# Dense 128-wide query and key products in a fused two-block attention kernel, with half of the x tiles transposed by DMA

## The chip, the cores and the metric

The kernel runs on one core of one Trainium2 chip. The metric is device time in microseconds (us) for one launch; a run's time is that of its slowest core, and here there is one. Engines are named as in the profile: PE (TensorE, matmuls; PEld its weight loads), ACT (ScalarE), DVE (VectorE), POOL (GpSimd) and SP (SyncE, which here only issues DMAs).

## The reference

Two independent blocks over 2048 tokens of width 640 with 32 heads of 20 dimensions; the outputs stand side by side.

```python
def _A_ref(x, wqkv, wo):                     # softmax attention
    qkv = (x @ wqkv).reshape(B, S, 3, H, Dh) # B=1, S=2048, H=32, Dh=20
    scores = einsum("bhqd,bhkd->bhqk", q, k) * Dh ** -0.5
    p = softmax(scores, axis=-1)
    o = einsum("bhqk,bhkd->bhqd", p, v)
    return o.reshape(B, S, D) @ wo           # D=640
def _B_ref(x, wqkv, wo):                     # linear attention
    phi = lambda t: where(t > 0, t + 1, exp(t)) + 1e-6
    kv = einsum("bhsd,bhse->bhde", phi(k), v); z = phi(k).sum(s)
    o = (phi(q) @ kv) / (phi(q) @ z + 1e-6)
    return o.reshape(B, S, D) @ wo
return concatenate([A, B], axis=-1)          # (1, 2048, 1280), bfloat16
```

## The kernel before

**Block A, the bulk.** The heads are taken in 8 groups of four, the queries in 4 chunks of 512 (qc), the keys in 16 tiles of 128 (kt). A block n is one query chunk and one group; there are 32, and n = 8 qc + g. The score of one head, 128 keys and 512 queries is a matmul of 32 rows (20 dimensions and padding) that fills one PSUM bank; four heads lie on the four row groups of PE and run side by side. There are 2048 such units. Most go to ACT, which takes the exponential of two banks at a time (`exp_op`, L1797, 128x1024, 746 instructions over PSUM banks 0 to 3); 556 of them go through DVE (L1695) and POOL (L1871), which form the exponential from three shifted integer copies. Then PE multiplies by V (`pv_emit`), DVE and POOL normalize (`norm`), small DMAs collect the heads (`f_OTd<-f_OTn`, L1919), and an output product follows.

**Projections.** Group 0 and group 1 (`_NP = 2`) have weights padded to 32 columns a head (`wqp`, `wkp`), so that their products (`step_qk0`) land in the layout that the scores want. The other 24 heads are computed 6 at a time, 120 columns wide (`_CH`, `step_qk`), evicted by DVE to a buffer `f_sq`, and each head is sent to its place by a DMA of 20 rows x 512 (L1175). So each 512 tokens take 2 + 4 products for queries and as many for keys: 48 in all, each of 5 quads (a quad is four matmuls of 32 columns side by side). x is needed transposed (`f_xT`): the 16 tiles of 128 tokens are loaded by four large DMAs and turned on PE (5 transposes a tile, L1031 and L949) with a copy by DVE or ACT behind (L1038, L1041, L1094).

**Block B** runs in PE's free time: its steps (`b_steps`) are held back by a pace, so that step k starts when a share between `B0` = 0.26 and `B1` = 0.92 of A's exponentials is scored. On ACT it has 52 exponentials (L1316). Its loads start in `begin`, once all K and V are there; `begin` makes DVE, ACT, POOL and SP wait (`barrier`) for the last users of the memory that it takes over.

**The order** is made when the program is built. `run` walks the engines along estimated times and emits what is ready; each engine then runs its list strictly in order, with semaphores between engines. On PE, `try_pe` tries a score burst first, then the step in hand, PV, more steps, and fillers that read zeros (`f_zt`). Score bursts may run at most two ahead of the exponentials. Projection steps wait in the list `qa` with a due block; those due within two blocks of the current one are urgent.

## Time and profile before

| quantity | value |
|---|---|
| median of 3 runs (lowest, highest) | 756.52 us (756.34, 756.85) |
| the profiled execution: time, span | 757.82 us, 755.7 us |
| busy: PE, ACT, DVE, POOL | 738.3, 712.1, 606.4, 584.2 us |
| mean granted clock of PE | 0.996 |

The span runs from the first to the last instruction; 2.1 us of the profiled execution lie around it. A busy share is a mean over stages, so the views of the rows below go by time: which engine idles when, and what it waits for.

### The profile page before, as it was taken

To read this page: it belongs to the slowest core of one execution; us is meant where nothing else is said; L and a number is where in the kernel's file an instruction comes from. 1 tells how busy PE (TensorE), PEld (TensorE's weight loads), DVE (VectorE), ACT (ScalarE), POOL (GpSimd) and SP (SyncE) were. 2 spreads that over 40 slices of the span, in tenths; PEclk is the share of its full clock that TensorE was granted. 3 is DMA by queue.
4 is the path that set the end of the run, shared out by engine and by line. 5 is a ranking of instruction groups with operands and counts; after the bars stand their busy time and mean duration, and the time that the engine had idled before them with its cause. 6 is when DMAs were issued, how large, how long until landed. Compare 5 with 4: busy or idle time off the path is not lost.

```text
span 755.7 us, 25131 instructions
## 1 busy us (share of the span) xinstructions
PE 738.3 (98%) x10955; PEld 263.4 (35%) x10955; DVE 606.4 (80%) x1158; ACT 712.1 (94%) x806; POOL 584.2 (77%) x344
## 2 busy tenths in 40 slices
PE   7999999999899999999999999999999999999996
PEld 4533442333223333333333333233233332333334
DVE  5788778877687788888888788798888787998982
ACT  4579889999999999999999999999999999999994
POOL 6468755779878788887879888877988878798781
PEclk9999999999999999999999999999999999999999
DMA  9101111105201002001000003020010100010001
GB/s 310 28 3 26 26 29 29 29 22 132 42 15 35 5 9 50 7 23 24 3 7 21 30 7 101 10 46 15 23 41 15 37 32 18 10 35 15 15 19 48
DMA packets 38494, 26.32 MB, mean 35 GB/s; under 512 B 21356, under 2 KB 38380, under 8 KB 38380
## 3 DMA queue, kind: packets, MB, share of 16 engines
q1 hardware_dynamic: 37068, 24.27, 11.6%
q8 instruction: 87, 1.43, 0.8%
q10 hardware_dynamic: 1312, 0.41, 0.2%
q14 instruction: 27, 0.22, 0.1%
HBM read 9.58 MB, written 5.24 MB: 20 GB/s over the span
## 4 chain that ended last, share of the span: by engine, by line
ACT 61%; PE 35%; DVE 2%; DMA 1%; POOL 0%; issue 0%; ACTq 0%; SPq 0%; DVEq 0%; POOLq 0%
ACT f_PT L1797 58%; PE ps L155 34%; ACT ps L1316 2%; DMA f_ar<-in_A_wqkv_dram 1%; DVE f_Sr L1695 1%; DVE f_KT L1118 0%; DVE f_xT L1094 0%; PE ps L949 0%; POOL f_Sr L1871 0%; DMA f_KT<-f_sq 0%; DVE f_ar L1350 0%; DVE f_V L1210 0%; DVE f_xT L1038 0%; DVE f_ar L1318 0%; DVE f_sq L1178 0%
## 5 line engine op out<-in xcount | busy, mean ns | idle before, releaser
L1797 ACT ACTIVATE f_PT<-ps 128x1024 bf16<-128x1024 f32 x746 | 698.3, 1128 | 29.6 <-PE ps L155 29.3
L1871 POOL TENSOR_SCALAR f_Sr<-f_Sr 128x2048 int16<-128x2048 int16 x278 | 527.5, 1898 | 108.4 <-PE ps L155 82.3
L1695 DVE TENSOR_SCALAR f_Sr<-ps 128x512 int16<-128x512 f32 x556 | 377.5, 684 | 77.0 <-PE ps L155 69.5
L155 PE MATMUL ps<-f_Qr,f_KT 32*128 32x512 bf16 x2048 | 293.4, 384 | 7.0 <-ACT f_PT L1797 3.6
L155 PEld LDWEIGHTS ps<-f_Qr,f_KT 32*128 32x128 bf16 x2048 | 74.1, 91 | 251.2 <-ACT f_PT L1797 227.6
L155 PE MATMUL ps<-f_ar 128*32 128x320 bf16 (+3 forms) x2496 | 156.1, 310 | 0.2
L155 PE MATMUL ps<-f_PT,f_V 128*21 128x512 bf16 x1492 | 142.8, 383 | 0.0
L155 PE MATMUL ps<-f_Sr,f_V 128*21 128x512 bf16 x1112 | 102.6, 382 | 0.0
L155 PEld LDWEIGHTS ps<-f_ar 128*32 128x32 bf16 (+1 forms) x2496 | 59.2, 95 | 69.1 <-issue 43.6
L1894 POOL TENSOR_TENSOR f_T<-f_T,f_Rt 128x512 bf16<-128x512 f32 x31 | 32.5, 1048 | 35.5 <-DVE f_Rt L1892 33.6
L155 PE MATMUL ps<-f_Sr,f_Vp 128*21 128x512 bf16 x556 | 54.5, 382 | 0.0
L155 PEld LDWEIGHTS ps<-f_PT,f_V 128*21 128x21 bf16 x1492 | 36.7, 90 | 46.2 <-issue 37.4
L1318 DVE SCALAR_TENSOR_TENSOR f_ar<-ps,f_ar 128x320 bf16<-128x320 f32 (+1 forms) x52 | 29.3, 563 | 12.5 <-ACT ps L1316 11.0
L155 PE MATMUL ps<-f_xT,f_ar 128*32 128x512 bf16 x480 | 37.4, 390 | 0.2
L155 PEld LDWEIGHTS ps<-f_Sr,f_V 128*21 128x21 bf16 x1112 | 25.6, 90 | 30.3 <-issue 20.3
L155 PE MATMUL ps<-f_ar,f_xT 128*32 128x160 bf16 x1280 | 34.8, 234 | 0.4 <-DVE f_Sr L1695 0.3
L1316 ACT ACTIVATE ps<-ps 128x320 f32<-128x320 f32 (+1 forms) x52 | 32.7, 629 | 0.0
L1314 DVE TENSOR_SCALAR f_ar<-ps 128x320 f32<-128x320 f32 (+1 forms) x52 | 28.8, 554 | 2.1 <-PE ps L155 2.1
L1901 DVE STREAM_TRANSPOSE f_T<-ps 128x512 f32<-128x512 f32 x32 | 22.7, 708 | 8.9 <-PE ps L155 8.7
L155 PEld LDWEIGHTS ps<-f_ar,f_xT 128*32 128x32 bf16 x1280 | 23.4, 96 | 14.4 <-issue 7.1
L155 PE MATMUL ps<-f_wo,f_OTd 120*32 120x320 bf16 x512 | 27.4, 302 | 0.0
L155 PE MATMUL ps<-f_xT,f_wq 128*32 128x512 bf16 (+1 forms) x320 | 24.6, 383 | 0.0
(78 smaller groups left out, 361.9 us busy)
## 6 DMA issues: line engine op xcount, KB each, us to landing
out_dram<-f_st SPq DMA_DIRECT2D x32, 160.0 KB
f_ar<-in_B_wqkv_dram SPq DMA_DIRECT2D x3, 800.0 KB
f_ar<-in_A_x_dram SPq DMA_DIRECT2D x3, 640.0 KB
f_Qr<-f_sq SPq DMA_DIRECT2D x96, 20.0 KB
f_KT<-f_sq SPq DMA_DIRECT2D x96, 20.0 KB
f_OTd<-f_OTn SPq DMA_DIRECT2D x96, 20.0 KB
f_ar<-in_A_wqkv_dram SPq DMA_DIRECT2D x2, 800.0 KB
f_wq<-in_A_wqkv_dram SPq DMA_DIRECT2D x1, 800.0 KB
```

The lines of the kernel that those rows point to most:

```text
L155: lambda e: e.matmul(out, lhsT, rhs, start=start, stop=stop, tile_position=tp, skip_group_check=sgc),
L1314: self.push("dve", lambda e: e.tensor_scalar(r1, src, 0.0, 1e-6, op0=ALU.max, op1=ALU.add), (("ps", b),), (rk,), _c_dve(n), prio=1, ok=ok, ...
L1316: "act", lambda e: e.activation(src, src, AF.Exp), (), (("ps", b),), _c_act(n), prio=0,
L1318: "dve", lambda e: e.scalar_tensor_tensor(dst, src, 1.0, r1, op0=ALU.min, op1=ALU.add),
L1695: post = lambda: self.push("dve", lambda e: e.tensor_scalar(self.Sr[:, s, i, :], self.ps[:, b, :], 0.0, 32639.0 - self.PH[-1], op0=ALU.max ...
L1797: return _Op("act", lambda e: e.activation(self.PT[:, s0:s0 + n, :], ps[:, b0:b0 + n, :], AF.Exp, scale=math.log(2.0) / 128.0, bias=self.l ...
L1871: return e.tensor_scalar(v, v, inc, 1.0, op0=ALU.add, op1=ALU.mult)
L1894: nmul, lambda e: e.tensor_tensor(T2v, Tv, R.unsqueeze(2).broadcast_to([128, 16, 32]), op=ALU.mult),
L1901: self.push("dve", lambda e: e.transpose(self.T[:], ps[:, b, :]), (("ps", b),), ("T",), 630, prio=-1, after=freed, ok=lambda: n == 0 or (" ...
```

## The change

Each 512 tokens now take five products of 128 columns for queries and five for keys, 40 in all. The first is a padded-weight product whose 12 spare columns of each of the four heads hold dimensions 80 to 127 (`_LO`): it is evicted twice, once masked (`km`) to its place and once to a buffer; the others are plain slices of the weights. Keys are collected over all 2048 tokens in a buffer `kq`, and one DMA per head piece (up to 20 rows x 2048, L1178) sends them on when the four token chunks of a slice are done; queries still go in pieces of 512. The block order gets one exchange (`NX = 1`, `od`): the second block is group 0 of the second query chunk. x tiles 8 to 15 come by ten DMA transposes on SP's queue (`XD = 2`); tiles 4 to 7 stay with PE. The output products of the first three query chunks take 5 slices of 128 instead of 6 of 120 (and padded ones), all groups collected by DMA. Block B's kv and num/den matmuls are written as quads. The weight copies at the start stand behind the copies of x, the start has 24 filler matmuls instead of 18, a rule (`PVH2`) puts due projection steps ahead of PV, and several constants of the order differ (B's pace 0.30 to 0.84).

```diff
-_CH = ((8, 14), (14, 20), (20, 26), (26, 32))
-_NP = 2
+_CH = ((128, 256), (256, 384), (384, 512), (512, 640))
+_NP = 1
+def _pieces(d0, d1):                    # (head, first row, rows, offset) of dimensions d0..d1
+_LO = [(h, r, m, 32 * i + 20 + a) for i in range(4) for h, r, m, a in _pieces(80 + 12 * i, 92 + 12 * i)]
...
-    DOUBLE = -4.0
+    DOUBLE = -6.0
+    NX = 1
+    XD = 2
+    HOT = 0
+    PVH2 = 9
-    B0 = 0.26
-    B1 = 0.92
-    LASTD = 2
+    B0 = 0.3
+    B1 = 0.84
+    LASTD = 9
-    DMIN = -7
-    PVHI = 9
+    DMIN = -5
+    PVHI = 11
-    DLEAD = 11
+    DLEAD = 10
...
+        od = [(qc, g) for qc in range(self.NQC) for g in range(N_GRP)]
+        for x in range(self.NX):
+            od.remove((x + 1, 0))
+            od.insert(x + 1, (x + 1, 0))
...  start_loads
-        xl(1)
-        xl(2)
+            for c in range(N_DC):
+                sch.dma("sp", lambda e, tc=tc, c=c: e.dma_start_transpose(
+                    self.xT[:, c, 512 * tc:512 * (tc + 1)], x2[512 * tc:512 * (tc + 1), 128 * c:128 * (c + 1)]),
+                    writes=(("xt", tc, c),))
...  consts
-        heat(14)
+        heat(16)
-            heat(4 if t == 3 else 0)
+            heat(8 if t == 3 else 0)
...  spread: keys of one head piece for all tokens
+                d = self.KT[32 * i + r:32 * i + r + m, g, :]
+                res = tuple(("K", h, x) for x in range(self.NQC))
...  stash: keys wait for the fourth token chunk
+            if self.kqc[ch] == self.NQC:
+                self.spread(which, 0, self.kq[k], tuple(("kq", k, x) for x in range(self.NQC)), ("k", u), plist)
...  begin
-                        ("wv", "wk", ("wst0", 0), ("wst0", 1)) + tuple(("wkp", g) for g in range(_NP)) + tuple(("xn", t) for t in range(4, self.NT)))
+                        ("wv", "wk", ("wst0", 0), ("wst0", 1)) + tuple(("wkp", g) for g in range(2)) + tuple(("kq", k, x) for k in range(2) for x in range(NQC)) + tuple(("xn", t) for t in range(4, 4 * self.XD)))
...  normed
-                    self.prio.append(self.step_out(t, h, range(6), needs=(("OTs", n - 2),), cb=odone))
+                    self.prio.append(self.step_out(t, h, range(5), needs=tuple(
+                        ("OTs", self.pos[qc, x]) for x in range(N_GRP)), cb=odone))
...  try_pe
+        if (self.cur is None and self.qa and self.qa[0].due <= self.nowA() + self.HOT
+                and self.aexp - 4 * self.apv < self.PVH2 and self.try_aux(t)):
+            return True
```

PE before, from the last scores of the second 512 keys to the first of the third (`f_id,f_ar` is a transpose of an x tile, `f_xT,f_ar 32x512` x20 a key product, `f_ar,f_xT` a V product, `f_Qr,f_KT` scores, `f_PT` and `f_Sr` PV, `f_zt` a filler).

```order
L155 MATMUL ps<-f_Qr,f_KT 128x512 x3
L155 MATMUL ps<-f_Sr,f_V 21x512 x4
L949 MATMUL ps<-f_id,f_ar 128x128 x10
L155 MATMUL ps<-f_PT,f_V 21x512 x4
L155 MATMUL ps<-f_zt 32x256
L155 MATMUL ps<-f_xT,f_ar 32x512 x20
L155 MATMUL ps<-f_Sr,f_V 21x512 x4
L155 MATMUL ps<-f_ar,f_xT 32x160 x40
L155 MATMUL ps<-f_Qr,f_KT 128x512 x6
```

PE after, the same place (`f_xT,f_wqp` is the query product of the second block).

```order
L155 MATMUL ps<-f_Qr,f_KT 128x512 x2
L155 MATMUL ps<-f_xT,f_wqp 32x512 x8
L155 MATMUL ps<-f_xT,f_ar 32x512 x20
L155 MATMUL ps<-f_ar,f_xT 32x160 x20
L155 MATMUL ps<-f_Sr,f_V 21x512 x4
L155 MATMUL ps<-f_PT,f_V 21x512 x4
L155 MATMUL ps<-f_ar,f_xT 32x160 x20
L155 MATMUL ps<-f_PT,f_V 21x512 x4
L155 MATMUL ps<-f_Qr,f_KT 128x512 x5
```

The transposes are gone from between the scores, and two fifths of a query product came in. SP's queue at the start, before:

```order
L969 DMA f_st<-in_A_x_dram 128x2x640 x2
L977 DMA f_ar<-in_A_x_dram 128x4x640
L984 DMA f_ar<-in_A_wqkv_dram 128x5x640
L977 DMA f_ar<-in_A_x_dram 128x4x640 x2
L987 DMA f_ar<-in_A_wqkv_dram 128x5x640
L988 DMA f_wq<-in_A_wqkv_dram 128x5x640
```

And after:

```order
L1008 DMA f_st<-in_A_x_dram 128x2x640 x2
L1016 DMA f_ar<-in_A_x_dram 128x4x640
L1023 DMA f_ar<-in_A_wqkv_dram 128x5x640
L1030 DMA_TRANSPOSE f_xT<-in_A_x_dram 128x512 x10
L1034 DMA f_ar<-in_A_wqkv_dram 128x5x640
L1035 DMA f_wq<-in_A_wqkv_dram 128x5x640
```

The two large x loads became ten transposes, and the key and query weights stand behind them. ACT's first exponentials, with the semaphores that each waits for, before:

```order
L1797 ACTIVATE f_PT<-ps 128x1024 [waits f_sem_pe] x33
L1797 ACTIVATE f_PT<-ps 128x1024
L1797 ACTIVATE f_PT<-ps 128x1024 [waits f_sem_pe] x189
L1797 ACTIVATE f_PT<-ps 128x1024
L1797 ACTIVATE f_PT<-ps 128x1024 [waits f_sem_pe] x3
```

And after:

```order
L1874 ACTIVATE f_PT<-ps 128x1024 [waits f_sem_pe] x33
L1874 ACTIVATE f_PT<-ps 128x1024
L1874 ACTIVATE f_PT<-ps 128x1024 [waits f_sem_pe] x129
L1874 ACTIVATE f_PT<-ps 128x1024 [waits f_sem_dma4,f_sem_dma3,f_sem_dma5,f_sem_dma2,f_sem_pe,f_sem_dma1,f_sem_dma0]
L1874 ACTIVATE f_PT<-ps 128x1024 [waits f_sem_pe] x59
```

Exponential 164 now also waits for six DMAs: they are the last key pieces, which `begin` waits for since their source `kq` lies in the memory that block B takes.

## Rows read from the trace of the kernel before

**Rows 1.** Page, part 1: busy us, share, instructions; then ACT by fortieths of span.
```profile
PE 738.3 (98%) x10955; PEld 263.4 (35%) x10955; DVE 606.4 (80%) x1158; ACT 712.1 (94%) x806; POOL 584.2 (77%) x344
...
ACT  4579889999999999999999999999999999999994
```

**Rows 2.** Timeline of ACT, 0 to 200 us: start, us, count, [idle before <-releaser].
```profile
13.55 5.61 ACT L1797 ACTIVATE f_PT<-ps 128x1024 bf16<-128x1024 f32 x6 [6.42 <-PE ps L155]
22.41 3.77 ACT L1797 ACTIVATE f_PT<-ps 128x1024 bf16<-128x1024 f32 x4 [3.25 <-PE ps L155]
29.43 5.63 ACT L1797 ACTIVATE f_PT<-ps 128x1024 bf16<-128x1024 f32 x6 [3.25 <-PE ps L155]
...
37.86 14.77 ACT L1797 ACTIVATE f_PT<-ps 128x1024 bf16<-128x1024 f32 x16 [2.81 <-PE ps L155]
56.41 29.58 ACT L1797 ACTIVATE f_PT<-ps 128x1024 bf16<-128x1024 f32 x32 [3.78 <-PE ps L155]
88.52 1.02 ACT L1797 ACTIVATE f_PT<-ps 128x1024 bf16<-128x1024 f32 x1 [2.53 <-PE ps L155]
90.02 15.74 ACT L1797 ACTIVATE f_PT<-ps 128x1024 bf16<-128x1024 f32 x17 [0.48 <-PE ps L155]
106.77 1.02 ACT L1797 ACTIVATE f_PT<-ps 128x1024 bf16<-128x1024 f32 x1 [1.01 <-PE ps L155]
110.54 84.80 ACT L1797 ACTIVATE f_PT<-ps 128x1024 bf16<-128x1024 f32 x92 [2.75 <-PE ps L155]
```

**Rows 3.** ACT's waits over the span: us in total, times, longest.
```profile
ACT f_PT L1797 <- PE ps L155: 29.3, 13, 6.4
ACT f_st L1258 <- PE ps L155: 4.9, 2, 4.4
```

**Rows 4.** Chain that ended last, in order of time: start, us, what.
```profile
42.60 46.22 PE ps L155 x822
...
108.18 1.89 DMA f_KT<-f_sq
...
701.36 41.27 ACT f_PT L1797 x45
...
742.68 7.69 PE ps L155 x163
```

**Rows 5.** Timeline of all engines, 0 to 40 us, PE and DVE rows.
```profile
7.01 0.36 DVE L1019 COPY f_ar<-f_ar 128x400 bf16<-128x400 bf16 x1 [1.88 <-DMA f_ar<-in_A_wqkv_dram]
...
8.22 2.26 PE L155 MATMUL ps<-f_xT,f_wqp 128*32 128x512 bf16 x20 [1.38 <-DVE f_xT L1038]
...
12.30 0.75 DVE L1118 TENSOR_SCALAR f_KT<-ps,f_kb 128x512 bf16<-128x512 f32 x1 [1.03 <-PE ps L155]
...
18.02 1.01 PE L949 MATMUL ps<-f_id,f_ar 128*128 128x128 bf16 x15
...
26.86 1.26 PE L155 MATMUL ps<-f_xT,f_ar 128*32 128x512 bf16 x20
27.95 0.39 PE L155 MATMUL ps<-f_Sr,f_V 128*21 128x512 bf16 x4
28.17 0.86 PE L155 MATMUL ps<-f_ar,f_xT 128*32 128x160 bf16 x40
28.99 0.62 PE L155 MATMUL ps<-f_Qr,f_KT 32*128 32x512 bf16 x6
```

**Rows 6.** Windows at the start and at 289 us; last three: clock, DMA share, GB/s.
```profile
9.00:10.00 1.00, 1.00 (x16) 0.49 (x12) 0.00 (x0) 0.00 (x0) 0.94 (x2) 0.50 1.08 365
...
289.00:290.00 1.00, 1.00 (x19) 0.21 (x11) 1.00 (x3) 1.00 (x3) 1.00 (x1) 1.00 0.58 131
```

**Rows 7.** Timeline of SP (DMA issues): start, us, count.
```profile
159.57 13.43 SPq L1175 DMA_DIRECT2D f_KT<-f_sq  x11
...
181.77 13.40 SPq L1293 DMA_TRANSPOSE f_ar<-in_B_x_dram  x10
```

**Rows 8.** Page, part 5: exponentials of block B on ACT: busy us, mean ns.
```profile
L1316 ACT ACTIVATE ps<-ps 128x320 f32<-128x320 f32 (+1 forms) x52 | 32.7, 629 | 0.0
```

More of the change, by code (lines that the diff above doesn't have):

```diff
@@ L1050, in wprep @@
     def wprep(self):
-        for j in range(_NP, 4):
+        for j in range(4):
+            if self.od[j][1] == 0:
+                continue
             self.push("pool", lambda e, j=j: e.tensor_copy(
@@ L1096, in step_x, with spread, after @@
         return _Step(mms, post, key=("xs", t), due=due)
+    def spread(self, which, tc, src, rs, k, plist):
+        self.sqturn[k] = len(plist)
+        for h, r, m, a in plist:
+            g, i = divmod(h, 4)
+            n = self.pos[tc, g]
+            if which == "Q":
+                d = self.Qr[32 * i + r:32 * i + r + m, n % 4, :]
+                res = (("Q", n % 4, i),)
+                keys = (("Q", n),)
+                okd = (lambda n=n: (n < 4 and ("Qi", n % 4) in self.done) or ("S", n - 4) in self.done)
+            else:
+                d = self.KT[32 * i + r:32 * i + r + m, g, :]
+                res = tuple(("K", h, x) for x in range(self.NQC))
+                keys = tuple(("K", g, x) for x in range(self.NQC))
+                okd = (lambda g=g: ("Ki", g) in self.done)
+            def after(keys=keys, g=g):
+                self.sqturn[k] -= 1
+                for key in keys:
+                    self.pieces[key] = self.pieces.get(key, 0) + 1
+                    if self.pieces[key] == _NPC[g]:
+                        self.done.add(key)
+            self.push("sp", lambda e, d=d, a=a, m=m: e.dma_start(d, src[a:a + m, :]), rs, res, 710,
+                      prio=n if which == "Q" else g, after=after, ok=okd)
@@ L1183, in step_qk @@
+                yield ("C", self.quad(b, 0, 512, w[:, c, d0:d1], self.xT[:, c, 512 * tc:512 * (tc + 1)],
+                                      c == 0, c == N_DC - 1, (nm,) + self.xt(tc)), 217.0)
+        def post(b):
+            self.stash(which, ch, tc, b)
         needs = ()
         if which == "Q" and tc > 0:
-            needs = (("S", tc * N_GRP + h0 // 4 - 4),)
-        if tc > 0:
-            needs += tuple(("xt", t) for t in range(4 * tc, 4 * tc + 4))
+            needs = (("S", self.pos[tc, h0 // 4] - 4),)
@@ L1188, in step_qk @@
+        needs += self.xtn(tc)
         return _Step(mms, post, key=("P", which, ch, tc), needs=needs, due=due)
@@ L1215, in post @@
                           (("ps", b), "Vones"), (("Vp", t, r),), _c_dve(w), prio=1, after=last)
-        return _Step(mms, post, key=key, due=due, needs=(("xt", t),) if t > 3 else ())
+        return _Step(mms, post, key=key, due=due, needs=(("xt", t),) if 0 < t // 4 < self.XD else ())
     @staticmethod
@@ L1241, in post @@
             self.done.add(("open", t, h))
-        return _Step(lambda b: self.out_mms(b, t, h, range(5)), post, needs=needs + ("wo",), key=("open", t, h))
+        return _Step(lambda b: self.out_mms(b, t, h, (0, 1, 2, 3, 5)), post, needs=needs + ("wo",), key=("open", t, h))
     def step_close(self, t, h):
@@ L1904, in normed @@
     def normed(self, n):
-        qc, g = divmod(n, N_GRP)
+        qc, g = self.od[n]
         self.done.add(("OTn", n))
         last = qc == self.NQC - 1
-        o = n % 3
-        if g < N_GRP - 2:
-            left = [4]
+        o = self.osl[n]
+        if g < N_GRP - 2 or not last:
+            pl = []
+            for i in range(4):
+                d0 = D_HEAD * (4 * g + i)
+                c0 = min(d0 + D_HEAD, 128 * (d0 // 128 + 1))
+                pl.append((i, d0, c0))
+                if c0 < d0 + D_HEAD:
+                    pl.append((i, c0, d0 + D_HEAD))
+            left = [len(pl)]
             def after():
@@ L2144, in run @@
             vs(tc, 0, 0)
-        self.qa.append(self.step_qk0("Q", 1, 0, 1))
-        for tc in range(NQC):
-            self.qa.append(self.step_qk0("K", 1, tc, 1))
+            if tc > 0 and self.pos[tc, 0] < 4:
+                self.qa.append(self.step_qk0("Q", 0, tc, 1))
         for ch in range(len(_CH)):
-            due = _CH[ch][0] // 4
+            g = _CH[ch][0] // (4 * D_HEAD)
+            due = self.pos[0, g]
             self.qa.append(self.step_qk("Q", ch, 0, due))
```

274 lines of the change are left out of this document (150 added, 124 removed).

## The prediction

> **What bounds the kernel now.** I read the page first: PE is busy for 98% of the span and ACT for 94% [rows 1], so the shares don't tell which of them sets the end. The fortieths do: ACT is at nine tenths or more from the eighth slice on, and below that only before and in the last [rows 1]. The timeline of ACT gives the places. Its first exponential starts at 13.55, and after that eight waits, each released by PE, take 3.25 + 3.25 + 2.81 + 3.78 + 2.53 + 0.48 + 1.01 + 2.75 = 19.9 us, the last of them ended at 110.54 [rows 2]. All waits of the exponentials for PE sum to 29.3 us, of which 6.42 is the first [rows 2, 3]; so beyond 111 us some 3 us are left. From there on ACT is the limit: 45 exponentials in a row take 41.27 us, 0.917 each [rows 4]. Up to 143 us the chain of waits runs mostly over PE (822 matmuls without a break from 42.60) [rows 4]. So PE is the bound of the first fifth, where all keys and values must be made beside the scores, and ACT is the bound of the rest. A microsecond of PE work saved early moves the end by as much; saved late, it moves nothing. The end itself, 13 us from 742.68, is PV, normalization and the last output products [rows 4].
>
> The change leaves ACT's list as it is: 746 exponentials of A and 52 of B (32.7 us busy [rows 8]). Hence the end moves by what ACT's idle time moves.
>
> **The start.** The first product begins at 8.22, after 1.38 us of waiting for DVE's x copies; these stand behind a weight copy at 7.01 that had waited for its DMA [rows 5]. After the change the x copies stand first. Against that, PE has six more fillers. Between 0 and 1.38 I take 0.6. In this stretch the granted clock fell to 0.50, that is 1.2 GHz, after the idle time ahead of it [rows 6], and 20 matmuls took 2.26 us where the same at 1.00 (2.4 GHz) take 1.26, or 1.09 from start to start [rows 5]. The two products, 8.22 to 12.30, would take about 2.35 instead of 4.08: 1.7 us, if the longer run of fillers keeps the clock (0 if it doesn't). I take both: **2.3 us**, bounds 0 and 3.1; first exponential near 11.2.
>
> **The waits for the next 512 keys** (the first three). The prices are: a product 1.09 (26.86 to 27.95), a PV quad 0.22 (27.95 to 28.17), 40 V matmuls 0.82 (28.17 to 28.99), a transpose 1.01/15 = 0.07 [rows 5].
> - Third 512 keys: the order before holds, between the scores, 10 transposes, one product, 40 V matmuls, three PV quads and a filler: 0.67 + 1.09 + 0.82 + 0.66 + 0.1 = 3.3 us. After: 8/20 of a product, a product, 40 V and three PV quads: 0.44 + 1.09 + 0.82 + 0.66 = 3.0. It also no longer waits for DVE's copies of the turned tiles. ACT's wait of 3.25 becomes about 2.5.
> - Second 512 keys: tiles 4 to 7 still go through PE, but 20 transposes stand between score bursts instead of 15 of them behind the last. Before, 0.22 + 1.01 + 0.22 + 0.1 + 1.09 + 0.82 = 3.5 us between scores; after, 0.22 + 1.09 + 0.82 + 0.22 = 2.35. The wait of 3.25 becomes 2.0.
> - Fourth: the scores go on while the key product is made; no stretch without scores is longer than 1.3 us, and two exponentials are in hand. 2.81 becomes 0.
>
> **The wait of 3.78.** Before it PE makes due key products for a stretch of 4.6 us by the prices; the order after has such a stretch of 4.6 at the same place (93 units scored, before 92). It stays: 3.8.
>
> **The last four waits** (6.8 us in all). Keys take 20 products instead of 24, and 40 transposes are gone: 4 x 1.09 + 40 x 0.07 = 7.2 us of PE work. Query products in the early part stay six, since one of the second chunk comes forward. Between 93 and 613 scored units the order after has no stretch over 1.6 us without scores; before, three such stretches led to these waits. But PE stays as full as ACT there: from unit 94 to 426 the order holds 112.6 us of PE work at these prices (a score burst with its two changes of form at 0.45), for 122 exponentials of 0.917, 111.9 us. I leave 1.5 us of waits for that, bounds 0 and 8.
>
> Sum: 19.9 - (2.0 + 2.5 + 0 + 3.8 + 1.5) = **10.1 us**.
>
> **A wait that is added.** `begin` makes ACT, DVE, POOL and SP wait for the last key pieces: exponential 164 stands behind six DMAs, and all of ACT's list behind it. Between the last key product and that exponential lie some 7 us of PE work. In that time DVE evicts (0.75 [rows 5]) and seven DMAs go out. Eleven such issues took 13.43 us, 1.22 each, with their own waits in it [rows 7]; a piece lands 1.89 us after its start [rows 4]. That is at most 0.75 + 8.5 + 1.9 = 11.2, a wait of 4; with issues of half the length none. I take **-1.2 us**.
>
> **Costed at nothing.** Fewer output quads (24 of 0.14) and query products later: ACT is the bound there. Block B's narrower pace: from unit 831 to 1742 the order holds 308 us of PE work at these prices, before 310 for about the same part, and ACT needs 911 units / 2.745 a burst x 0.917 = 304 us and some 13 for block B: PE keeps 9 us in hand. The ten transposes: below. More, smaller DMAs for outputs and queries on SP: they have a block of slack. The end has the same list: 13 us.
>
> Total 2.3 + 10.1 - 1.2 = 11.2 us: the span goes from 755.7 to 744.5. The profiled execution took 757.82, 1.3 above the median of 756.52; I take the difference from the median: 756.5 - 11.2 = **745.3 us**.
>
> **Rivals.**
> - *PE stays the bound to 200 us.* The two limits lie within a microsecond of each other from unit 94 on, and waits of one for the other add up. For it: PE ran 46 us without a break there and ACT still waited [rows 2, 4]. Against: 7 us less work. With 8 us lost instead of 1.5 and half of the start, about 752; middle 750.
> - *Nearly all early waits go.* If the stretches shrink to what two exponentials in hand cover, only the 3.8 stays: 2.7 + 16 - 1 = 17.7, so 739.
> - *The transposes come late* (ends slower). PE is in order: the third key product waits for five transposes, the fourth for ten, with all scores behind. By the prices these are reached at about 24 and 27 us. Ten transposes passed SP in 13.40 us [rows 7], so from 3 us on until 16.4, landing near 19: 8 us of slack. While five were under way the DMA share was 0.58 at 131 GB/s; at the start the plain loads have it full, at 365 GB/s [rows 6], so they will be slowed. Each microsecond over 27 is lost; beyond 38, some 2.7 times the length of [rows 7], the kernel is slower than before. At three times, 46 us: 19 lost, 764.
>  The Trainium skill (VectorE: DVE Perf Modes, "The three transpose paths" and the rules) advises TensorE for a 128x128 transpose and gives 1309 ns a tile by DMA: 40 tiles one after another would be 52 us, and by that rule this rival is the outcome, near 773. The trace speaks against it: 40 tiles in 13.40 us, 0.34 each [rows 7].
> - *Key pieces come late* (slower too). A group's keys leave only when all 2048 tokens are done, behind query pieces on SP that wait for scores. One late piece cost 2.75 us before (1.89 of it the DMA) [rows 2, 4]. Six later groups at that price are 16.5: 762; from the fifth on the gain is gone. Against it: a product list that runs a block ahead.
> - *The change moves ACT's idle time without removing it*: B packed more tightly gives the waits back in the middle. Within 0.2%, 756.
>
> **Chances.** Forecast 0.55 (742 to 748), PE the bound 0.18, nearly all gone 0.12, transposes late 0.06, key pieces late 0.05, moved only 0.04. A difference under 0.2% (1.5 us) can't be told from none. Faster 0.85, same 0.04, slower 0.11. The range takes the first three: 739 to 753.
>
> **What would show it.** In the profile after: first exponential near 11.2 and a clock that doesn't fall between 8 and 12 us; ACT's waits in the first 60 us near 2, 2.5, 0 and 3.8; no wait over 1 us from there to exponential 164, and there one of 0 to 4 that names DMA or a DVE row behind it; the third and fourth key product not released by a DMA; a chain of waits that passes to ACT before 60 us; the last 13 us as before. Wrong would make it: a PE wait for `f_xT` from a DMA, ACT waits between 200 and 740 that sum to over 5 us, or PE's row in the chain still the largest up to 140 us.

## The result and the profile after

The changed kernel takes 746.56 us (median of six runs, 744.05 to 749.18) against 756.68 us before: a ratio of 0.985, with a 95% interval of 0.982 to 0.988. The forecast of 745.3 us is 1.3 us off, and the measurement lies in the range. The profiled execution took 747.08 us with a span of 745.3; before it was 757.82 and 755.7. So there are 10.4 us of span to account for.

The page first: part 1, and from part 2 the fortieths of ACT and of the granted TensorE clock.

```profile
PE 724.1 (97%) x11201; PEld 253.8 (34%) x11201; DVE 602.5 (81%) x1150; ACT 712.3 (96%) x806; POOL 585.7 (79%) x345
...
ACT  4879999998989999999999999999999999999994
...
PEclk9999999999979999999999999999999999999999
```

ACT works as long as before (712.3 us, before 712.1 [rows 1]), so the end moved by what its idle time moved. The shares say no more than that. The fortieths show the places: ACT stays at nine tenths from the fourth slice on, before from the seventh, but for two slices, the tenth (168 to 186 us) and the twelfth (205 to 224 us), the latter beside a granted clock of 0.7. The timeline of ACT has the waits themselves (start, us, count, [idle before <-releaser]); it answers to [rows 2]:

```profile
11.16 5.68 ACT L1874 ACTIVATE f_PT<-ps 128x1024 bf16<-128x1024 f32 x6 [4.17 <-PE ps L155]
18.75 3.77 ACT L1874 ACTIVATE f_PT<-ps 128x1024 bf16<-128x1024 f32 x4 [1.90 <-PE ps L155]
24.77 1.94 ACT L1874 ACTIVATE f_PT<-ps 128x1024 bf16<-128x1024 f32 x2 [2.25 <-PE ps L155]
26.97 18.82 ACT L1874 ACTIVATE f_PT<-ps 128x1024 bf16<-128x1024 f32 x20 [0.26 <-PE ps L155]
49.54 130.46 ACT L1874 ACTIVATE f_PT<-ps 128x1024 bf16<-128x1024 f32 x142 [3.75 <-PE ps L155]
180.61 1.02 ACT L1874 ACTIVATE f_PT<-ps 128x1024 bf16<-128x1024 f32 x1 [0.61 <-PE ps L155]
182.43 1.02 ACT L1874 ACTIVATE f_PT<-ps 128x1024 bf16<-128x1024 f32 x1 [0.80 <-PE ps L155]
...
207.88 3.02 ACT L1874 ACTIVATE f_PT<-ps 128x1024 bf16<-128x1024 f32 x3 [0.76 <-PE ps L155]
...
231.51 2.85 ACT L1874 ACTIVATE f_PT<-ps 128x1024 bf16<-128x1024 f32 x3 [1.26 <-PE ps L155]
```

Read from the top: the first exponential comes at 11.16 instead of 13.55. The eight waits of [rows 2], 19.9 us, have become 1.90 + 2.25 + 0.26 + 3.75 = 8.2. From 49.54 on 142 exponentials run without a wait to 180 us. Then nine waits come that the kernel before did not have in this size: 6.0 us in all from 180 to 232 us, where the kernel before has one of 0.6 (and one of 1.3 at 240 us). Behind that, one wait of 0.30 is left up to the tail. The sum for the exponentials (us, times, longest; [rows 3] has 29.3, 13 and 6.4):

```profile
ACT f_PT L1874 <- PE ps L155: 18.6, 15, 4.2
```

So the account is: 13.55 - 11.16 = 2.4 us at the start, 19.9 - 8.2 = 11.7 up to 180 us, and 6.3 - 3.0 = 3.3 lost behind it. That gives 10.8 us where the span has 10.4; the difference of 0.4 is not itemized (ACT's busy time, for one, is 0.2 us longer). The three terms are used below for every version, all from the timeline of ACT: the first exponential, its waits from there to 180 us ("early"), and all its waits for PE, DVE and POOL from 180 us to the tail ("late").

| version | median us | first exponential | early | late |
|---|---|---|---|---|
| before | 756.7 | 13.55 | 19.9 | 3.0 |
| after | 746.6 | 11.16 | 8.2 | 6.3 |
| start as before | 749.3 | 11.33 | 8.4 | 5.9 |
| wk and wq ahead of the transposes | 747.3 | 11.13 | 9.3 | 7.2 |
| tiles 8 to 15 on TensorE | 776.9 | 11.19 | 17.1 | 27.0 |
| no exchange of blocks | 778.8 | 11.01 | 20.4 | 24.3 |
| eight products more | 796.1 | 11.02 | 15.7 | 46.5 |
| seven numbers as before | 774.4 | 11.79 | 9.6 | 34.7 |
| PVHI alone as before | 788.8 | 11.01 | 9.6 | 46.4 |
| both: seven numbers as before, tiles on TensorE | 772.6 | 11.06 | 14.9 | 25.9 |
| block B's pace alone as before | 754.0 | 11.77 | 8.2 | 13.6 |
| mask comparisons on POOL | 751.2 | 11.19 | 8.9 | 11.9 |
| late fillers | 742.8 | 11.79 | 8.2 | 3.2 |
| late fillers, not issued | 745.7 | 11.31 | 8.9 | 4.3 |

The chain of waits (start, us, what), which answers to [rows 4]:

```profile
39.43 52.42 PE ps L155 x888
...
108.38 45.90 PE ps L155 x809
...
697.58 34.85 ACT f_PT L1874 x38
732.48 7.56 PE ps L155 x172
```

It still runs over PE up to 154 us, although ACT does not wait at all from 49.54 us on: up to 180 us both are full. The chain steps back to whatever released an instruction, and where two engines are full it can stay with either. The tail from 732.48 is 12.8 us, before 13.0.

### The profile page after: what moved, and what is told of

It reads as the page before. It is cut to its first block, busy times and chain, and to the rows that moved or that the text cites. A ratio compares the mean times of both kernels' runs of the same rounds, so it can differ in the third digit from the quotient of the medians.

```text
span 745.3 us, 25679 instructions
## 1 busy us (share of the span) xinstructions
PE 724.1 (97%) x11201; PEld 253.8 (34%) x11201; DVE 602.5 (81%) x1150; ACT 712.3 (96%) x806; POOL 585.7 (79%) x345
## 4 chain that ended last, share of the span: by engine, by line
ACT 55%; PE 37%; DVE 3%; DMA 2%; SPq 1%; issue 1%; DVEq 0%; ACTq 0%
ACT f_PT L1874 52%; PE ps L155 37%; ACT ps L1392 3%; DMA f_ar<-in_A_wqkv_dram 1%; DVE f_Sr L1772 1%; SPq L2004 1%; SPq L1178 1%; DVE f_ar L1423 0%; PE ps L988 0%; DMA f_OTd<-f_OTn 0%; DMA f_KT<-f_ar 0%; DVE f_OTn L1975 0%; DVE f_KT L1239 0%; DVE f_ar L1394 0%; DVE f_T L1978 0%
## 5 line engine op out<-in xcount | busy, mean ns | idle before, releaser
L155 PE MATMUL ps<-f_ar 128*32 128x320 bf16 (+4 forms) x3024 | 151.2, 295 | 1.7 <-DVE f_Sr L1772 0.6
L155 PEld LDWEIGHTS ps<-f_ar 128*32 128x32 bf16 x3024 | 60.5, 95 | 65.3 <-issue 36.2
L155 PE MATMUL ps<-f_ar,f_xT 128*32 128x160 bf16 x1280 | 37.8, 234 | 1.3 <-DMA f_ar<-in_A_wqkv_dram 0.7
L155 PE MATMUL ps<-f_wo,f_OTd 128*32 128x320 bf16 (+1 forms) x608 | 31.9, 302 | 0.8 <-DMA f_OTd<-f_OTn 0.6
L155 PE MATMUL ps<-f_xT,f_ar 128*32 128x512 bf16 x400 | 30.6, 383 | 0.4 <-DVE f_xT L1152 0.2
L1286 DVE CAST f_V<-ps 128x160 bf16<-128x160 f32 x64 | 19.5, 316 | 8.9 <-PE ps L155 8.8
```

Of the source, the lines that this page charges most:

```text
L155: lambda e: e.matmul(out, lhsT, rhs, start=start, stop=stop, tile_position=tp, skip_group_check=sgc),
L1286: self.push("dve", lambda e: e.tensor_copy(dst, src), (("ps", b), "Vones"), (("V", t, r),), _c_dve(w), prio=1, after=None if isd else last)
```

## The experiments

**Where the new waits from 180 to 232 us come from.** Here is the stretch around 205 us in the kernel after, from the timeline of all engines (start, us, count, [idle before <-releaser]):

```profile
202.50 3.87 POOL L1948 TENSOR_SCALAR f_Sr<-f_Sr 128x2048 int16<-128x2048 int16 x2 [1.53 <-PE ps L155]
...
204.72 1.75 DVE L1423 TENSOR_SCALAR f_ar<-f_ar 128x147 bf16<-128x147 int32 x1
...
205.35 0.39 PE L155 MATMUL ps<-f_Qr,f_KT 32*128 32x512 bf16 x3
206.39 0.67 DVE L1772 TENSOR_SCALAR f_Sr<-ps 128x512 int16<-128x512 f32 x1
...
207.12 0.39 PE L155 MATMUL ps<-f_zt 128*32 128x256 bf16 x2 [1.38 <-DVE f_Sr L1772]
```

L1423 is one of ten comparisons that build block B's mask. Seven of the ten take 0.17 to 0.24 us; this one takes 1.75 and ends at 206.47, 0.1 us after the second POOL instruction (202.50 + 3.87 = 206.37). Another ends at 179.21, POOL's at 179.11. The Trainium skill ("SBUF — State Buffer", "SBUF: two separate sides") says that the port pair that VectorE and GpSimd share is a lock held for a whole instruction; the two ends agree with that. DVE's exponential behind it is late, and PE stands 1.38 us. What it stands on is a filler (`f_zt`), put into the bank that DVE has not read yet, with a burst of scores queued behind it. A window of the same kernel behind it (columns as in [rows 6]: busy time of PE, PEld, DVE, ACT, POOL, then granted clock, DMA share, GB/s):

```profile
212.00:214.00 2.00, 2.00 (x17) 0.38 (x15) 0.07 (x1) 1.42 (x2) 1.92 (x2) 0.50 0.07 21
```

From 208 to 219 us the clock is at 0.50, the 1.2 GHz level; a score burst takes 0.61 us instead of 0.39 and ACT works 1.42 us out of 2.

One version below ("start as before") has the same order of PE here, the same slow comparison and the same gap, but there the clock stays at 1.00. Its gap and ACT's wait behind it, from the timeline:

```profile
207.37 0.39 PE L155 MATMUL ps<-f_zt 128*32 128x256 bf16 x2 [1.38 <-DVE f_Sr L1772]
...
208.13 19.36 ACT L1874 ACTIVATE f_PT<-ps 128x1024 bf16<-128x1024 f32 x21 [0.75 <-PE ps L155]
```

And the stretch behind it as a window, in the kernel after:

```profile
208.00:219.00 11.00, 11.00 (x76) 2.18 (x68) 5.23 (x8) 8.87 (x9) 10.52 (x7) 0.53 0.03 7
```

And in that version:

```profile
208.00:219.00 11.00, 10.14 (x108) 2.97 (x109) 7.64 (x13) 10.87 (x12) 10.52 (x7) 1.00 0.03 7
```

So the gap alone costs ACT 0.75 us, and the fallen clock 2.0 us more (8.87 us of work instead of 10.87). The gap does not bring the fall by itself; what else decides was not found.

In the kernel after, two explanations were open: the comparisons on DVE start all of it ("port"), or PE simply has too little to do there ("empty").

*Mask comparisons on POOL.*

```diff
-                        self.push("dve", lambda e: e.tensor_scalar(
+                        self.push("pool", lambda e: e.tensor_scalar(
                             mf[:, 0:21 * nh], it[:, 0:21 * nh], 0.0, None, op0=ALU.is_le),
...
-                                "dve", lambda e: e.tensor_scalar(
+                                "pool", lambda e: e.tensor_scalar(
                                     mg[:, 0:21 * nh], it[:, 0:21 * nh], -19.0, None, op0=ALU.is_ge),
```

> Edit to the changed kernel: the ten small comparisons that build block B's mask (five pairs, 128x147 or 128x168, SBUF to SBUF) run on POOL instead of DVE. In the changed kernel two of them took 1.77 us instead of 0.23 and ended 0.1 us after the POOL instruction that ran beside them (179.21 against 179.11 us, 206.47 against 206.37); behind them DVE's exponentials were late, PE stood 1.36 and 1.38 us, the granted clock fell to 0.50 (181 to 184 and 208 to 219 us), and ACT waited eight times, 4.8 us in all, between 180 and 220 us. Theory 'port': these comparisons start the chain. Then no wait of ACT over 0.5 us between 170 and 225 us, no granted clock under 0.95 there, about 742 us (746.6 - 4.8), and the executions lie closer together than 744.05 to 749.18. Rival 'empty': the clock falls because PE has too little to do between A's projections and block B (PE busy 8.07 of 10 us at 200 to 210), whatever DVE does: dips and waits of 3 to 5 us stay in this stretch, 745 to 748 us.

Measured: 751.19 us (749.84 to 753.85), and the dip is still there. PE in the timeline, then a window:

```profile
181.95 0.40 PE L155 MATMUL ps<-f_Sr,f_V 128*21 128x512 bf16 x4 [1.53 <-POOL f_Sr L1948]
```

```profile
184.00:188.00 4.00, 4.00 (x24) 0.94 (x23) 1.39 (x3) 3.42 (x4) 3.84 (x3) 0.50 0.47 105
```

"Port" as I had put it falls: without the comparisons on DVE the gap on PE is 1.53 us, now released by POOL, which spends 0.59 us on each comparison and comes late with its own step of the exponentials. The clock falls behind this gap too (0.50 from 183 to 193 us), and then not again up to the tail. The remaining loss, five waits between 541 and 725 us, 7.5 us in sum, belongs to the subject below.

*Late fillers.*

```diff
-            if self.est("pe", (), (("ps", x),)) <= t:
+            if self.est("pe", (), (("ps", x),)) <= t - 800.0:
```

> Edit to the changed kernel: a filler product (32 columns of zeros, only there to keep PE busy) goes only into a PSUM bank that has been free for 0.8 us by the plan, instead of one that is free now. In the changed kernel PE's waits for DVE (3.3 us in 6) lie ahead of fillers that were put into a bank which a late DVE exponential still held, with score bursts queued behind them; the plan now has 96 such fillers, before 95. Theory 'port': the fillers hand DVE's lateness on to ACT. Then PE's waits for f_Sr fall from 3.3 to under 1 us, ACT's waits at 180 and 207 us to under 1 us in sum unless the clock still falls, 743 to 745 us. Rival 'empty': what holds the filler holds the next score of DVE too, or fewer products at that place let the clock fall sooner: 746 to 749 us with dips as long.

Measured: 742.75 us (742.16 to 743.59), 0.980 of the kernel before (0.977 to 0.983). The comparison on DVE is as slow as ever, and PE still waits, but half as long, and now on a PV matmul (timeline, then a window):

```profile
203.51 1.79 DVE L1423 TENSOR_SCALAR f_ar<-f_ar 128x147 bf16<-128x147 int32 x1
...
206.79 0.39 PE L155 MATMUL ps<-f_Sr,f_V 128*21 128x512 bf16 x1 [0.76 <-DVE f_Sr L1772]
```

```profile
208.00:212.00 4.00, 3.96 (x42) 1.17 (x41) 2.73 (x5) 4.00 (x5) 3.84 (x3) 1.00 0.04 10
```

The clock stays at 1.00 through the whole stretch, ACT's waits from 180 to 300 us fall from 6.0 to 2.9, and the five runs lie within 1.4 us instead of 5. So the filler turned a short lateness of DVE into a long gap of PE; where the gap is shorter, the clock stayed up to the tail, and the mean clock of all five runs is 0.998 to 0.999. The falls make most of the difference between the medians: the fastest run of the kernel after, at 0.998, has a span of 742.2 us, and the runs of this version have 740.4 to 741.7. "Port" holds in the main, with two misses: PE's waits for `f_Sr` fall from 3.3 to 2.0 us and not to under 1, and ACT's two waits sum to 1.42. This version is faster than both kernels.

*Late fillers, not issued*: the last version once more, the fillers planned but left out, so that the order of everything else stays.

```diff
-                                  reads=("zt",), writes=(("ps", self.PVB),), tp=(0, 0))], 110.0)
+                                  reads=("zt",), writes=(("ps", self.PVB),), tp=(0, 0), skip=True)], 110.0)
...
-        m = dict(out=self.ps[0:32, b, 0:256], l=zt[:, 0:32], r=zt[:], tp=(0, 0))
+        m = dict(out=self.ps[0:32, b, 0:256], l=zt[:, 0:32], r=zt[:], tp=(0, 0), skip=True)
...
+            if m.get("skip"):
+                continue
```

> Edit to the version with the late fillers (742.75 us, spans 740.4 to 741.8, granted clock 1.00 from 160 to 240 us): the fillers behind the start are not issued; the order of everything else on all engines is the same. In that stretch PE then works some 0.7 us out of 0.92 around each exponential, without anything between. Theory 'gap': what let the clock fall in the changed kernel were idle stretches of PE of over 1 us; single gaps here stay under 1 us except at the two late comparisons on DVE, so the clock may fall there once or twice; 742 to 747 us. Theory 'empty': without fillers PE has too little to do all through 165 to 235 us, and the clock stays at 0.50 for 30 us or more; products of 0.61 us instead of 0.39 then make ACT wait as at 208 to 219 us (2.4 us in 10): 748 to 757 us. Rival 'fillers only harm': clock and time as without the edit or better, 741 to 743 us.

Measured: 745.65 us (744.04 to 747.51), 2.9 more than with them. Windows of this version:

```profile
172.00:176.00 4.00, 2.94 (x31) 0.70 (x28) 3.69 (x8) 4.00 (x5) 1.55 (x5) 1.00 0.46 167
176.00:180.00 4.00, 3.45 (x28) 0.67 (x28) 3.02 (x8) 3.30 (x5) 2.39 (x2) 0.57 1.05 248
...
192.00:196.00 4.00, 4.00 (x28) 0.74 (x27) 2.28 (x4) 3.77 (x5) 3.11 (x4) 0.50 0.13 33
```

The time fits "gap" (the range I gave holds it), its mechanism does not: no wait of PE is longer than 0.7 us here, yet the clock falls three times between 176 and 232 us, behind stretches in which PE waits about 0.5 us ahead of every second score burst. "Empty" fits no better, since the clock also comes back between them. What the rows bear out is the weaker statement that idle time of PE, in one piece or in many, came before each fall, and not that each such stretch brings one. The fillers are worth 2.9 us where they stand in this version. Where they stand in the kernel after, no gain is left of them: it takes 746.56 us against 745.65 here without any, and the runs of the two overlap (744.05 to 749.18 and 744.04 to 747.51). The kernel after without its own fillers was not run.

**The start.** *Start as before*: weight copies ahead of the x copies again, 14 and 4 fillers.

```diff
+        for k, (wp, nm) in enumerate(((self.wqp, "wqp"), (self.wkp, "wkp"))):
...
-        heat(16)
+        heat(14)
...
-            heat(8 if t == 3 else 0)
+            heat(4 if t == 3 else 0)
...
-        for k, (wp, nm) in enumerate(((self.wqp, "wqp"), (self.wkp, "wkp"))):
```

> Edit to the changed kernel: the start as before: the copies of the first weights stand ahead of the x copies on DVE and POOL, and 14 and 4 fillers instead of 16 and 8. Forecast: this part is worth 2.3 us (0.6 of waiting for DVE and 1.7 of a clock at 0.50 between 8 and 12 us): first exponential at 13.4 instead of 11.2, granted clock 0.50 at 9 to 10 us, 748 to 749 us. Rival 'swallowed': the first waits for keys have ends of their own (loads and copies that come by their own time), so a later start shortens them: first exponential near 13.4, but the waits behind it shorter by 1 to 2 us, 746 to 747 us. Rival 'clock alone': the x copies come as early as now, since the weight loads do, and only the clock falls: first exponential at 12.5 to 13.

Measured: the first exponential at 11.33, 0.17 us later than after, which is within the spread of the versions that share the start of the kernel after (11.01 to 11.79). None of the three views had that. DVE and PE of this version, from the timeline of all engines:

```profile
6.06 0.36 DVE L1068 COPY f_ar<-f_ar 128x400 bf16<-128x400 bf16 x1 [1.05 <-DMA f_ar<-in_A_wqkv_dram]
6.34 0.88 DVE L1091 COPY f_xT<-ps 128x640 bf16<-128x640 bf16 x2
...
7.27 1.26 PE L155 MATMUL ps<-f_xT,f_wqp 128*32 128x512 bf16 x20 [0.57 <-DVE f_xT L1091]
```

The order is that of [rows 5], where the same copy began at 7.01. Here its weights are there at 6.06, PE waits 0.57 instead of 1.38, and 20 matmuls take 1.26 us: the clock has not fallen. What is left of the change at this place is the first weight load, which is a fifth smaller (128 columns instead of 160). The transposes in place of plain loads are not the cause: with tiles 8 to 15 loaded plainly, POOL's copy of the same weights also runs at 6.08 (before 7.03). Two clearings of the weight buffers on DVE, of 0.59 us each, are gone as well, but before the change they ended at 2.35, ahead of DVE's wait for the load. That the size of the load is the cause follows by exclusion; it was not tried alone. The median of 749.3 us is no loss inside the kernel: this version's spans (744.5 to 747.6) are those of the kernel after (742.2 to 747.4), but 3.8 to 4.3 us of its time lie outside the span, in the others about 1.8, and 2.1 before the change. No run here tells why.

**What the transposes cost by their lateness.** *wk and wq ahead of the transposes*: SP's queue alone.

```diff
+        sch.dma("sp", lambda e: e.dma_start(self.wk, awq[:, :, D_MODEL:2 * D_MODEL]), writes=("wk",))
+        sch.dma("sp", lambda e: e.dma_start(self.wq[:], awq[:, :, 0:D_MODEL]), writes=("wq",))
         for tc in range(1, self.NQC):
...
-        sch.dma("sp", lambda e: e.dma_start(self.wk, awq[:, :, D_MODEL:2 * D_MODEL]), writes=("wk",))
-        sch.dma("sp", lambda e: e.dma_start(self.wq[:], awq[:, :, 0:D_MODEL]), writes=("wq",))
```

> Edit to the changed kernel: the loads of wk and wq (1.6 MB) stand ahead of the ten transposes in SP's queue instead of behind them; the order on every other engine is the same. In the changed kernel the DMA engines carry 71 to 124 GB/s from 13 to 17 us, 108 to 128 from 20 to 22, and 339 to 392 from 22 to 25: so the transposes end near 22 us, and wk and wq follow. Ahead of the transposes, wk and wq take some 4.5 us at those rates. Forecast ('8 us of slack' before the fourth key product at 26, and the third at 21.8): the transposes' five for the third product end some 4 us later than now, about 20 to 21, the last five near 26: PE waits 0 to 1 us, 745 to 748 us. Rival 'tight': transposes keep only their own rate and the plain loads hold them up longer than 4.5 us: PE waits for f_xT from DMA 3 us or more ahead of the third or fourth product, ACT as much, and the end is 3 to 6 us later.

Measured: 747.25 us (742.84 to 749.38). SP and PE in the timeline:

```profile
4.96 20.12 SPq L1032 DMA_TRANSPOSE f_xT<-in_A_x_dram  x10
...
27.05 0.62 PE L155 MATMUL ps<-f_xT,f_ar 128*32 128x512 bf16 x8 [0.95 <-DMA f_xT<-in_A_x_dram]
```

The ten transposes leave SP at 25.08 instead of 19.62, 5.5 us later, and PE then waits 0.95 us ahead of the fourth key product; ACT's fourth wait grows from 0.26 to 1.26. The forecast of 745 to 748 us holds. By these rows the slack in the kernel after is an estimated 4.5 us (5.5 - 0.95), and the 0.95 us beyond it came through to ACT as 1.0.

**What the parts are worth.** *Tiles 8 to 15 on TensorE.*

```diff
-    XD = 2
+    XD = 4
```

> Edit to the changed kernel: x tiles 8 to 15 are loaded plainly and turned on TensorE again (40 transposes and 8 copies on DVE), the exchange and the five products stay. Theory of the forecast ('products'): the 40 transposes cost 0.07 us each on a PE that is the bound there, 2.8 us, and some 0.5 us of DVE copies ahead of a key product: 749 to 751 us, with the third and fourth wait for keys 0.5 to 2 us longer. Rival 'order': since the exchange leaves PE slack, most of the 2.8 us is hidden and the waits for the next 512 keys change by under 0.7 us each: 745 to 748 us. A third outcome, transposes by DMA slower than PE's (they hold up wk and wq): faster than 745 us.

Measured: 776.88 us (776.68 to 777.19), more than any view had. ACT's timeline:

```profile
27.72 5.78 ACT L1874 ACTIVATE f_PT<-ps 128x1024 bf16<-128x1024 f32 x6 [5.17 <-PE ps L155]
...
57.29 22.11 ACT L1874 ACTIVATE f_PT<-ps 128x1024 bf16<-128x1024 f32 x24 [6.43 <-PE ps L155]
```

Early it loses 8.9 us where I had 3 to 4, and 20.7 us more behind 180 us.

*No exchange of blocks.*

```diff
-    NX = 1
+    NX = 0
```

> Edit to the changed kernel: the exchange of blocks is undone (the second block of A takes the next four heads of the first 512 queries again); five dense products and transposes by DMA stay. Theory of the forecast ('products'): the gain of the first 110 us came from fewer products and transposes on PE; the exchange only brought two fifths of a query product forward. Then ACT's waits in the first 60 us change by under 1 us, those from 60 to 170 us stay near 0, and it takes 746 to 749 us. Rival 'order': the second block on the same keys and values puts the second group of keys off by a block, and this took away the waits behind due key products (3.78 at 56 us and 6.8 us in four to 111 us). Then 4 to 10 us of waits return between 45 and 115 us: 751 to 757 us.

Measured: 778.79 us (776.26 to 781.3). PE and ACT in the timeline:

```profile
35.61 4.49 PE L155 MATMUL ps<-f_xT,f_ar 128*32 128x512 bf16 x80
...
44.65 0.38 PE L155 MATMUL ps<-f_Qr,f_KT 32*128 32x512 bf16 x1 [1.85 <-DMA f_KT<-f_ar]
...
45.06 1.02 ACT L1874 ACTIVATE f_PT<-ps 128x1024 bf16<-128x1024 f32 x1 [8.69 <-PE ps L155]
...
51.99 1.94 ACT L1874 ACTIVATE f_PT<-ps 128x1024 bf16<-128x1024 f32 x2 [5.90 <-PE ps L155]
```

"Order" holds: the next heads' keys are due as soon as the first block ends. Four key products stand in a row, and then PE waits for the pieces that SP's DMAs spread, 1.85 and 1.83 us. Behind each of these two waits the granted clock was at 0.50 for 3.4 us; behind the first, the next key product took 2.36 us instead of 1.26. So the rival "key pieces late" of the forecast makes 3.7 us of ACT's two waits of 8.69 and 5.90; the products in a row and the clock come on top, and were not told apart. The exchange, 12.2 us early, is what keeps all of it away. From 60 to 170 us the waits stay at 1.2 and 0.55 us, as "products" had it. The total is more than either view had, by the late loss.

*Eight products more*, whose results nobody reads.

```diff
+                if ch < 2:
+                    self.qa.append(self.step_extra(ch, tc, due))
```

> Edit to the changed kernel: eight more products of 20 matmuls (32x512, as a key product, 1.09 us each, 8.7 us in all) whose results nobody reads, one behind each key product of the second and third chunk, due with them. They add PE work alone: no eviction, no DMA. Theory of the forecast ('products'): PE work of the first 110 us moves the end by as much, or as little as 1.5 us of it hidden: waits of 6 to 9 us are added before 165 us, and 752 to 757 us, more if late waits follow. Rival 'slack': PE is as full as ACT there, but work runs ahead of its due time by a block, so most of the 8.7 us is taken out of the fillers after 165 us: under 3 us added before 180 us, 745 to 749 us.

Measured: 796.07 us (795.48 to 796.17). New early waits, from ACT's timeline:

```profile
111.01 1.02 ACT L1886 ACTIVATE f_PT<-ps 128x1024 bf16<-128x1024 f32 x1 [2.95 <-PE ps L155]
...
135.87 1.03 ACT L1886 ACTIVATE f_PT<-ps 128x1024 bf16<-128x1024 f32 x1 [2.14 <-PE ps L155]
138.66 28.61 ACT L1886 ACTIVATE f_PT<-ps 128x1024 bf16<-128x1024 f32 x31 [1.77 <-PE ps L155]
```

8.7 us of PE work add 7.6 us of early waits: there the forecast's exchange rate, nearly one for one, is shown. But 40 us more are lost late, in stretches that have none of the added products, and the total lies outside both views.

The rule `PVH2`, the output products in slices of 128 and block B's quads were not tried alone.

**The late loss.** In three versions more was lost behind 180 us than before it, and never in the kernel after. The change's seven numbers that set the order were the suspects.

*Seven numbers as before.*

```diff
-    DOUBLE = -6.0
+    DOUBLE = -4.0
...
-    B0 = 0.3
-    B1 = 0.84
-    LASTD = 9
+    B0 = 0.26
+    B1 = 0.92
+    LASTD = 2
...
-    DMIN = -5
-    PVHI = 11
+    DMIN = -7
+    PVHI = 9
...
-    DLEAD = 10
+    DLEAD = 11
```

> Edit to the changed kernel: seven numbers that set the order go back to their values before (block B's pace 0.26 and 0.92, LASTD 2, DMIN -7, PVHI 9, DLEAD 11, DOUBLE -4). Theory of the forecast ('nothing'): they cost and bring nothing, since ACT is the limit where they act: 745 to 748 us, with the list to 160 us as it is. Rival 'fit': they set when DVE's and POOL's share of the exponentials is made, and the second half hangs on it. With the exchange or the transposes undone and these numbers kept, waits of 5 to 6 us came between 550 and 705 us, each in a stretch in which PE did PV of f_Sr, then 16 of f_PT, and no scores. Then such waits of 3 us or more appear here too: over 750 us.

*The same with the tiles on TensorE* (both edits together).

> Edit to the changed kernel: x tiles 8 to 15 on TensorE again, and the same seven numbers at their values before. With the tiles alone undone it took 776.9 us: ACT's waits to 180 us summed to 16.7 us from the first exponential on, against 8.2, and those after 500 us to some 22, against 0. Theory 'fit': the late loss is due to numbers that fit another order; with those that were made for transposes on TensorE it goes, and what is left is the early loss: 746.6 + 8.5, 752 to 758 us. Rival 'follows': the late waits follow from the early ones, whatever the numbers: 768 us or more.

*PVHI alone as before* and *block B's pace alone as before*.

```diff
-    PVHI = 11
+    PVHI = 9
```

> Edit to the changed kernel: one number alone goes back, PVHI from 11 to 9 (PE goes on with a product that it has begun as long as fewer than so many exponentials lie unread ahead of PV, and else does PV first). With seven numbers back it took 774.4 us. Theory 'one number': PVHI carries most of the 28 us, since with 9 products wait for PV and DVE's and POOL's exponentials fall behind at the ends of the blocks; waits of 3 to 9 us between 400 and 740, each with f_Sr, f_Vp products some 2 us apart and 16 of f_PT behind: 765 us or more. Rival 'pace': block B's pace carries it, and this edit gives 745 to 750 us.

> Edit to the changed kernel: block B's pace alone goes back, from 0.30 to 0.84 to 0.26 to 0.92. Theory 'one number' (PVHI): 746 to 755 us, with late waits of under 10 us in sum. Rival 'pace': 765 us or more, with waits of 5 us and more between 540 and 700. The forecast's own view ('nothing'): 745 to 748 us.

Measured: seven numbers 774.4 us (773.08 to 778.09), the same with the tiles on TensorE 772.6 (772.16 to 773.06), PVHI alone 788.8 (788.31 to 790.24), the pace alone 754.0 (751.43 to 755.29). Two of these, the pace alone and both edits together, do not compute the reference: their output has a relative error of 0.17. They have as many instructions on ACT and POOL as the kernel after, so their times say what such an order takes, but neither is a kernel to use, and what in the order spoils the output was not found.

For the seven numbers "fit" holds against "nothing", and for PVHI "one number": by itself it is worth 42 us in this arrangement, more than the whole set with 28, so the numbers don't add up. The pace is worth 7.5, within what "one number" had, with late waits of 13.6 us in place of under 10. For the tiles "fit" failed, and "follows" came true: numbers that were set with transposes on PE bring back only 4 of 30 us, so that loss isn't a matter of these numbers alone. Read the other way, with the old numbers the transposes by DMA bring nothing (774.4 us with them, 772.6 without).

What such a late wait looks like, in the version with PVHI at 9 (timeline of all engines):

```profile
562.27 9.81 POOL L1948 TENSOR_SCALAR f_Sr<-f_Sr 128x2048 int16<-128x2048 int16 x5 [1.03 <-PE ps L155]
...
568.40 1.29 PE L155 MATMUL ps<-f_zt 128*32 128x256 bf16 x7
570.16 0.40 PE L155 MATMUL ps<-f_Sr,f_Vp 128*21 128x512 bf16 x4 [0.47 <-POOL f_Sr L1948]
...
573.36 1.04 PE L155 MATMUL ps<-f_PT,f_V 128*21 128x512 bf16 x16 [0.51 <-DVE f_T L1978]
...
573.80 3.77 ACT L1874 ACTIVATE f_PT<-ps 128x1024 bf16<-128x1024 f32 x4 [8.20 <-PE ps L155]
```

At a block's end POOL has five steps of the exponentials to do in a row (1.96 us each), PV of that block can only go on as each is done, and nothing but fillers lies between. The four quads of the next block (16 matmuls of `f_PT`) that would free ACT's buffers come when the block is closed; till then ACT stands 8.20 us. The row names PE as the releaser, but PE itself waits for POOL. And POOL had time earlier in the same block. Its rows ahead of those five steps:

```profile
546.44 1.90 POOL L1948 TENSOR_SCALAR f_Sr<-f_Sr 128x2048 int16<-128x2048 int16 x1 [1.00 <-PE ps L155]
549.69 1.90 POOL L1948 TENSOR_SCALAR f_Sr<-f_Sr 128x2048 int16<-128x2048 int16 x1 [1.35 <-PE ps L155]
552.74 1.90 POOL L1948 TENSOR_SCALAR f_Sr<-f_Sr 128x2048 int16<-128x2048 int16 x1 [1.15 <-PE ps L155]
559.34 1.90 POOL L1948 TENSOR_SCALAR f_Sr<-f_Sr 128x2048 int16<-128x2048 int16 x1 [4.69 <-DVE f_sq L1202]
```

With the 1.03 us ahead of the five, POOL stood 9.2 us in this block, more than the 8.20 that ACT then lost. So in this block the share of the exponentials that DVE and POOL make was fed too late. The score gaps of 5 to 8 us in the other slow versions end in the same way, with 16 matmuls of `f_PT` behind products of `f_Sr`, but in most of them PE does products of block B in between and not fillers; POOL's part was followed in this version alone. Why a PVHI of 9 leads to late feeding, step by step through the rules that set the order, was not followed.

## Why the prediction was right

- **What bounds the kernel.** Right: PE early, ACT behind (ACT is at nine tenths from the seventh slice on, not the eighth). Eight more products cost 7.6 us early for 8.7 us of work; ACT's busy time did not change.
- **The start, 2.3 us.** Right in size (2.4), wrong in its cause. The two effects that I added up are there: PE no longer waits 1.38 us, and the clock doesn't fall. But the order of the copies and the longer fillers bring at most 0.17 us of it, which is within the spread of the start. The step "x copies stand behind a weight copy that had waited for its DMA" looked at the order, not at the size of that load.
- **The first three waits**, 3.25 to 2.0, 3.25 to 2.5 and 2.81 to 0: measured 1.90, 2.25 and 0.26. **The 3.78 that stays**: 3.75. Right; counting what the order holds between two score bursts was good to 0.3 us each.
- **The last four waits**, 6.8 to 1.5: they went altogether. PE and ACT are as full as I had found, but being equally full made no waits. The version without the exchange agrees that fewer products and transposes do this: its waits from 60 to 170 us stay small too.
- **The added barrier, -1.2**: nothing. Exponential 164 lies inside the run of 142 without a wait (33 to 174). The six pieces were not late.
- **Costed at nothing, the rest.** This step failed. In the kernel after it hides a loss of 3.3 us (fillers behind a late DVE, and a clock at 0.50 for some 13 us in all). With late fillers the late waits are 3.2 us, before 3.0, so these two make up the loss. It was offset by the 1.5 and 1.2 us above, which I had put too high: that the total came within 1.3 us is in this part luck. And the zero isn't a property of this work: with one number at its old value the same work costs 42 us, with the whole set 28. I had compared sums (308 us of PE work against 317 on ACT) and taken PE's 9 us in hand as cover. That says nothing on when DVE's and POOL's share is fed, and that is what decided in the block that was followed.
- **The transposes.** Right that they are in time. My 19 us for the landing came from [rows 7]; at the start ten of them took 16.79 us on SP instead of 13.40, and the data rates point to 22. The slack was about 4.5 us, not 8. (And the kernel would have been slower than before from some 2.4 times the length of [rows 7], by the other numbers of that sum, not 2.7.) The Trainium skill (VectorE: DVE Perf Modes, "The three transpose paths") gives 1309 ns for one 128x128 tile by DMA. As a price for tiles in a row it isn't borne out: 40 tiles passed SP in 16.79 us, 0.42 each; no run here has a tile by itself.
- **Key pieces late.** Rightly unlikely, but the reason I gave ("a product list that runs a block ahead") is the exchange of blocks, which I had credited with two fifths of a product. Without it PE waits 1.85 and 1.83 us for late pieces, inside a loss of 12.2 us.
- **PE stays the bound to 200 us.** There was a loss up to 232 us, of another kind and at another place.
- **The signs.** Two of those that I named for "wrong" need a word. PE's row in the chain is the largest up to 154 us, though ACT does not wait: as a sign it was badly chosen, since with two full engines the chain may follow either. The waits of ACT's exponentials between 200 and 740 us sum to 4.4 us, just under the 5 that I had set; a wait of 4.3 that ends at 738.57 belongs to the tail, as one of 4.45 did before.

The sum: 2.3 + 10.1 - 1.2 = 11.2 forecast, 2.4 + 11.7 - 3.3 = 10.8 found.

## What to carry to other kernels

Work that is costed at nothing because an engine has time in hand over a long stretch is covered only if the engines that feed each other are fed in time: in this kernel it was not covered whenever they were fed late. Look for the last consumer at each block's end (here PV behind POOL), not at sums. Where a plan made by rules and numbers sets the order, a part undone with the numbers kept does not show what the part is worth: read such an experiment up to the first place where the plan itself goes astray, and give the rest as a separate account. A filler belongs in a buffer that has been free for a while, since in an in-order queue it hands a neighbour's lateness on to all that stands behind it.

## What was not expected of the hardware

- The granted TensorE clock fell to 0.50 in the middle of the kernel, behind single gaps of 1.38 us (after) and 1.53 us (comparisons on POOL), and behind many of 0.5 us in a third version; behind gaps of 0.76 us (late fillers) and 0.87 us (before) it stayed. It also stayed behind the same gap of 1.38 us in two versions (start as before, at 207 us, and block B's pace alone, at 209). It came back after 3 to 14 us. The runs of the kernel after spread with it: clock 0.998 with a span of 742.2 us, 0.984 with 747.4.
- Ten transposes of 512x128 took SP 13.40 us before, 16.79 at the start of the kernel after, and 20.12 with 1.6 MB of plain loads ahead of them.
- A comparison of 128x147 elements on DVE took 1.75 us instead of 0.24 where a POOL instruction of 1.90 had begun 0.24 us ahead of it, and ended 0.1 us behind that one.
